# The dense rhythm of the channel-mixing units starts at step 84 instead of step 88

## The chip, the cores and the metric

The kernel runs on one core of a Trainium2 chip. A core has a matrix engine (TensorE, PE in the profile, with its weight loads as PEld), a vector engine (VectorE, DVE), a scalar engine (ScalarE, ACT), a general engine (GpSimd, POOL) and an engine that issues transfers (SyncE, SP). They run side by side and wait for each other through semaphores. Sixteen DMA engines move the data. The metric is the device time of one execution in microseconds.

## What is computed

Three blocks follow each other, for a batch of B = 4 sequences of S = 448 tokens:

```python
attn = softmax(mask(q @ k.T / sqrt(64))) @ v          # 12 heads of 64 columns -> x of 768 columns
h  = relu(x.T @ w_tok1) @ w_tok2                      # token mixing, 448 -> 256 -> 448
u  = x + h.T
x2 = u + relu(u @ w_ch1) @ w_ch2                      # channel mixing, 768 -> 1536 -> 768
theta = x2 @ w_theta                                  # third block
y  = w_tok_r @ (x2 * cos(theta)) + w_tok_i @ (x2 * sin(theta))
out = (x2 + y) + relu((x2 + y) @ w_ch)
```

The inputs are 64-bit floats. Large products are made as three products of a high and a low part (`mm3`, lines 170 to 172), so that little precision is lost.

## The kernel before

**Attention is a loop of 168 steps.** The 12 heads of a batch make 6 pairs, the 4 batches 24 pairs, and a pair has 7 tiles of scores. Step `n` is tile `n % 7` of pair `n // 7`. A step issues `scores` (PE products at L274 and L276, the masked minimum on DVE at L281, the exponential on ACT at L283) and then `late_step(n - 4)`, the product with v of the tile of four steps before.

**The probabilities are transposed in one of two ways.** For pairs 0 to 11 (`NATPV`, steps 0 to 83) PE transposes them through the identity (L290), ACT copies them out of PSUM (L292), and PE multiplies in 32 bits (L318). For pairs 12 to 23 (steps 84 to 167) ACT and DVE split them into two 16-bit parts (tile `ph`, 3 buffers, L111 and L303), SP issues a DMA transpose into tile `pt` (L306), and PE multiplies in 16 bits (L329). PE has less to do in such a step.

**Token mixing.** When two pairs are done, `finish` scales their output and splits it (`xg`, L111 on ACT and L118 on DVE), and one step later `tokmix` runs (L354 to L356, L363, L365, and `mm3` on `wt`). It belongs to the attention's own chain. The last one of a batch makes the columns `acc`, which are split into `ut` for channel mixing.

**Channel mixing is cut into 96 units**, 24 for each batch: 6 units `ch1_unit` and 6 units `ch2_unit` for each half of the 1536 columns. A unit is 18 products of 128x128 by 448 columns (L170 to L172, with `ws` as the weights; `ut` or `h` as the other operand), and its result leaves PSUM through ACT and DVE (L387, L388) or DVE (L396). Units are the filler between the steps of attention: the list `UNIT_STEPS` says behind which step each unit is issued. From unit 0 at step 46 there is one unit each 3 steps (14 in 42), and from step 88 on 29 units in 42 steps. Units that the loop has not issued follow after it: one, then the last token mixing, then all but the last 16, and those between the loading of the third block's weights.

**The weights of a unit** fill a tile `ws` of 768 KB (4 buffers). For units 0 to 23 they must be converted from 64-bit floats first, a *rounding*: SP fetches `raw` (768 KB, 2 buffers, L124), ACT takes the absolute value (L127), DVE assembles the 32-bit value (L134, L135, L137, L138), ACT and DVE split it into `ws` (L111, L118), and SP stores it (`w_c<-ws`, L448). `ROUNDINGS` says at which step: by hand for the even units from 14 on and a few others (`AHEAD_STEPS`, long before their unit), and otherwise at `UNIT_STEPS[n] - 5`, so that the tile goes straight into its unit. A rounding's first part is issued behind the scores of its step, and the rest, the store and the fetch for the next rounding but one, behind those of the step after. All other weights, those of units 24 to 95 among them, are streamed back from memory (`ws<-w_c`, L165) by `load_unit`, called for the next two units after each unit.

```python
        for j, (at_step, _) in enumerate(ROUNDINGS):
            if at_step == n - 1:
                with tc.issue_after(pairs[b, pr].first.ins):
                    round_rest(j)
...
        if n >= LAG:
            with tc.high_priority(AHEAD):
                late_step(n - LAG)
...
        run_units(sum(at_step == n for at_step in UNIT_STEPS))
    for n in range(len(steps) - LAG, len(steps)):
        late_step(n)
    run_units(1)
```

Scores and `late_step` are issued at a high priority. A planner orders the instructions of each engine from the program's order, the priorities and its own costs; on the chip each engine then works in that order.

Of the kernel before, what the change touches and what calls it, by code (L numbers as in the profile page):

```python
# [31 lines left out]
AHEAD, LAG, LOOK = 500, 4, 2  # L32
KEEP, UBACK = 6, 16
LATE_CONVERT = 16
FIRST_UNIT, PHASE, RATES = 46, 42, (14, 29)
UNIT_STEPS = [FIRST_UNIT + -(-n * PHASE // RATES[0]) if n < RATES[0] else
              FIRST_UNIT + PHASE + -(-(n - RATES[0]) * PHASE // RATES[1]) for n in range(72)]
AHEAD_STEPS = {0: 18, 1: 22, 2: 26, 3: 30, 4: 34, 5: 38, 14: 43, 16: 47, 18: 51, 20: 55, 22: 70}
ROUNDINGS = sorted([(at_step, n - 4) for n, at_step in enumerate((3, 4, 8, 9))] +
                   [(AHEAD_STEPS.get(n, UNIT_STEPS[n] - 5), n) for n in range(24)])  # L40
ENGINES = {
# [12 lines left out]
def fused(ctx, tc, q, k, v, w_tok1, w_tok2, w_ch1, w_ch2, w_theta, w_tok, w_ch, out):  # L54
# [353 lines left out]
    def load_unit(n):  # L408
        if n < len(units) and n not in loaded and (n >= 24 or n in stored):
            b, fh, c, t = units[n]  # L410
            loaded[n] = stream_tile(wd[f"c{c}", fh, t])
# [50 lines left out]
    def run_units(n):  # L462
        for _ in range(n):
            u = at[0]
            load_unit(u)
            b, fh, c, t = units[u]
            if c == 1:
                ch1_unit(b, uTs[b], fh, t, loaded[u])
            else:
                ch2_unit(b, uTs[b], accs[b], fh, t, loaded[u])  # L470
            loaded[u] = None
            at[0] += 1
            for ahead in range(LOOK + (u >= 24)):
                load_unit(at[0] + ahead)
            split_ready()
# [31 lines left out]
    for n, (b, pr, t) in enumerate(steps):  # L507
# [27 lines left out]
        if n == FIRST_UNIT - 4:  # L535
            load_unit(0)
            load_unit(1)
        run_units(sum(at_step == n for at_step in UNIT_STEPS))
    for n in range(len(steps) - LAG, len(steps)):
# [247 lines left out]
```

## Time and profile before

| | |
|---|---|
| device time, median of 3 runs | 929.29 us (927.43 to 929.35) |
| profiled execution, span from the first to the last instruction | 924.1 us |
| profiled execution, its own device time | not recorded beside the span; the median lies 5.2 us above the span |
| PE busy | 900.6 us (97%) |
| DVE busy | 633.5 us (69%) |
| ACT busy | 388.2 us (42%) |
| 16 DMA engines, queue of SP | 67.9% |
| mean granted clock of PE | 0.996 of full |

Busy shares are means over the whole span. PE's matmuls are pipelined, so that the duration of one (0.37 us) is longer than its distance to the next (0.20 us). A wait is shown with what released it.

### The profile page before, as it was taken

Reading aid. Unit: us, or ns where it says so; the run is one execution under the profiler, and the core shown is the slowest. Engines: PE = TensorE matmul, PEld = TensorE weight load, DVE = VectorE, ACT = ScalarE, POOL = GpSimd, SP = SyncE. Lnnn points to the kernel's source line nnn. Section 1 sums busy time; section 2 is a strip of 40 time slices with the busy share of each in tenths; the row PEclk is TensorE's granted clock in tenths of the full one; section 3 lists DMA queues with packets and bytes.
Section 4 is the critical chain, followed back from the end, with each engine's and each line's share of the span. In section 5 each row is a group of like instructions: output and inputs, shape, how many; then the busy total and the mean of one; then the engine's idle time right before and its main releaser. Section 6 shows DMA issues by size and latency. Waiting matters only on the chain.

```text
span 924.1 us, 15928 instructions
## 1 busy us (share of the span) xinstructions
PE 900.6 (97%) x5820; PEld 825.6 (89%) x5820; DVE 633.5 (69%) x1468; ACT 388.2 (42%) x914; POOL 109.9 (12%) x177
## 2 busy tenths in 40 slices
PE   7999999997999999999999999999999999999998
PEld 5988999896898898989899999999999999999997
DVE  6799797998987777467774288845864566575341
ACT  6788677675655555344532144321211212202100
POOL 2110000000000000000000000021631233242120
PEclk9999999998999999999999999999999999999999
DMA  6677994789999979699797899864505225054033
GB/s 184 190 254 254 360 335 172 251 300 272 260 316 317 285 207 263 223 275 290 199 322 244 280 326 369 281 195 132 184 1 162 78 86 179 19 162 128 6 133 129
DMA packets 104687, 199.17 MB, mean 216 GB/s; under 512 B 60896, under 2 KB 72992, under 8 KB 104608
## 3 DMA queue, kind: packets, MB, share of 16 engines
q1 hardware_dynamic: 103296, 196.35, 67.9%
q0 software_dynamic: 1152, 1.57, 0.9%
q8 instruction: 46, 0.75, 0.3%
q14 instruction: 33, 0.27, 0.1%
q10 hardware_dynamic: 160, 0.23, 0.1%
HBM read 149.36 MB, written 34.60 MB: 199 GB/s over the span
## 4 chain that ended last, share of the span: by engine, by line
PE 81%; DMA 10%; DVE 6%; issue 1%; ACT 1%; SPq 1%; ACTq 0%; DVEq 0%
PE ps_mm L170 18%; PE ps_mm L172 18%; PE ps_mm L171 18%; DMA pt<-ph 6%; PE ps_sc L274 3%; PE ps_sc L172 3%; PE ps_sc L170 3%; PE ps_sc L171 3%; PE ps_pv L318 3%; PE ps_pv L329 3%; DMA raw<-in_w_ch_dram 2%; PE ps_mm L290 2%; PE ps_sc L276 1%; PE ps_mm L355 1%; PE ps_mm L356 1%
## 5 line engine op out<-in xcount | busy, mean ns | idle before, releaser
L170 PE MATMUL ps_mm<-h,ws 128*128 128x448 f32 x432 | 159.4, 370 | 2.1 <-DMA ws<-w_c 1.3
L171 PE MATMUL ps_mm<-h,ws 128*128 128x448 f32 x432 | 159.2, 369 | 0.0
L172 PE MATMUL ps_mm<-h,ws 128*128 128x448 f32 x432 | 158.6, 368 | 0.0
L172 PE MATMUL ps_mm<-ut,ws 128*128 128x448 f32 x288 | 106.4, 369 | 0.0
L170 PE MATMUL ps_mm<-ut,ws 128*128 128x448 f32 x288 | 106.3, 369 | 0.0
L171 PE MATMUL ps_mm<-ut,ws 128*128 128x448 f32 x288 | 105.9, 368 | 0.0
L283 ACT ACTIVATE sb<-sb,mx 128x192 f32<-128x192 f32 (+3 forms) x168 | 89.3, 532 | 32.4 <-DVE mx L281 31.4
L170 PEld LDWEIGHTS ps_mm<-h,ws 128*128 128x128 f32 x432 | 81.2, 188 | 9.7 <-DMA ws<-w_c 1.6
L172 PEld LDWEIGHTS ps_mm<-h,ws 128*128 128x128 f32 x432 | 81.2, 188 | 7.0
L171 PEld LDWEIGHTS ps_mm<-h,ws 128*128 128x128 f32 x432 | 81.2, 188 | 6.8
L281 DVE CUSTOM_DVE_ANT_0 sb<-ps_sc,mask 128x192 f32<-128x192 f32 (+3 forms) x168 | 74.2, 455 | 10.2 <-PE ps_mm L290 5.8
L114 POOL TENSOR_SCALAR ut<-acc 128x448 fp32r<-128x448 f32 x24 | 17.4, 731 | 474.9 <-PE ps_mm L171 454.3
L591 ACT ACTIVATE tmp<-ps_sc 128x384 f32<-128x384 f32 x28 | 13.5, 482 | 132.3 <-PE ps_sc L172 132.1
L303 DVE SCALAR_TENSOR_TENSOR ph<-sb,ph 128x64 f16<-128x64 f32 (+3 forms) x156 | 42.8, 318 | 33.2 <-ACT ph L111 32.4
L318 PE MATMUL ps_pv<-v_raw,ptf 128*128 128x128 f32 (+1 forms) x456 | 63.6, 275 | 1.4 <-issue 0.9
L318 PEld LDWEIGHTS ps_pv<-v_raw,ptf 128*128 128x128 f32 x456 | 59.6, 192 | 5.7 <-issue 2.3
L111 ACT ACTIVATE ph<-sb 128x192 f16<-128x192 f32 (+3 forms) x84 | 36.5, 443 | 66.9 <-DMA pt<-ph 66.5
L172 PEld LDWEIGHTS ps_mm<-ut,ws 128*128 128x128 f32 x288 | 54.2, 188 | 4.5 <-issue 0.2
L170 PEld LDWEIGHTS ps_mm<-ut,ws 128*128 128x128 f32 x288 | 54.2, 188 | 4.5 <-issue 0.2
L171 PEld LDWEIGHTS ps_mm<-ut,ws 128*128 128x128 f32 x288 | 54.2, 188 | 4.2
L388 DVE SCALAR_TENSOR_TENSOR h<-ps_mm,h 128x448 fp32r<-128x448 f32 x48 | 29.7, 619 | 31.3 <-ACT h L387 31.2
L598 ACT ACTIVATE tmp<-tmp 128x384 f32<-128x384 f32 x28 | 14.7, 526 | 86.0 <-DVE tmp L596 86.0
(152 smaller groups left out, 2113.7 us busy)
## 6 DMA issues: line engine op xcount, KB each, us to landing
ws<-w_c SPq DMA_DIRECT2D x107, 768.0 KB, 5.5
raw<-in_w_ch_dram SPq DMA_DIRECT2D x30, 768.0 KB, 6.3
w_c<-ws SPq DMA_DIRECT2D x30, 768.0 KB, 6.6
q_raw<-in_q_dram SPq DMA_DIRECT2D x16, 448.0 KB, 5.3
k_raw<-in_k_dram SPq DMA_DIRECT2D x16, 448.0 KB, 6.3
v_raw<-in_v_dram SPq DMA_DIRECT2D x24, 288.0 KB, 4.9
x2d<-acc SPq DMA_DIRECT2D x24, 224.0 KB, 4.8
acc<-x2d SPq DMA_DIRECT2D x24, 224.0 KB, 3.6
```

What stands on the lines that cost most here:

```text
L111: nc.scalar.activation(dst, src, AF.Copy, scale=scale)
L170: nc.tensor.matmul(ps, lhsT=ka(a[:, 0]), rhs=kb(b[:, 0]), start=first, stop=False)
L171: nc.tensor.matmul(ps, lhsT=ka(a[:, 0]), rhs=kb(b[:, 1]), start=False, stop=False)
L172: return nc.tensor.matmul(ps, lhsT=ka(a[:, 1]), rhs=kb(b[:, 0]), start=False, stop=last)
L274: nc.tensor.matmul(ps[:, 0:n], lhsT=lhs, rhs=cut(pp.kh), start=True, stop=pp.kl is None)
L281: pp.first = nc.vector.tensor_tensor_reduce(out=dst, in0=src, in1=msk, op0=ALU.add, op1=ALU.min, scale=-0.125, scalar=3.0e38, accum_out=pp ...
L283: pp.last = nc.scalar.activation(sb[:, 0:kk], sb[:, 0:kk], AF.Exp, bias=pp.mx[:, j:j + 1], scale=-1.0, accum_out=pp.sm[:, j:j + 1])
L290: nc.tensor.transpose(pst[:, u * P:(u + 1) * P], full[:, c0 + u * P:c0 + (u + 1) * P], ident)
L303: nc.vector.scalar_tensor_tensor(out=dst, in0=sb[:, c0:c1], scalar=PSC, in1=hi[:, c0:c1], op0=ALU.mult, op1=ALU.subtract)
L318: pp.pv = nc.tensor.matmul(pp.ps[:, reg:reg + n], lhsT=pt[:, u], rhs=pp.v[0][:, vt * D:vt * D + n], start=(u == 0), stop=(u == len(blks) - 1))
L329: pp.pv = nc.tensor.matmul(pp.ps[:, reg:reg + D], lhsT=pt[:, blk], rhs=pp.v[c][:, vt * D:(vt + 1) * D], start=(n == 0), stop=(n == len(job ...
L388: gates[0] = nc.vector.scalar_tensor_tensor(out=t[:, 1], in0=ps[:, 0:S], scalar=0.0, in1=f32v(t[:, 0]), op0=ALU.max, op1=ALU.subtract)
```

## The change

The list of steps is made in another way. The sparse part stays one unit each 3 steps from step 46, now for 13 units; the dense part begins at step 84, the first step of pair 12, and spreads units 13 to 69 evenly over steps 84 to 167.

```diff
-FIRST_UNIT, PHASE, RATES = 46, 42, (14, 29)
-UNIT_STEPS = [FIRST_UNIT + -(-n * PHASE // RATES[0]) if n < RATES[0] else
-              FIRST_UNIT + PHASE + -(-(n - RATES[0]) * PHASE // RATES[1]) for n in range(72)]
+FIRST_UNIT, SPLIT_FROM, STEPS, EVERY = 46, 84, 168, 3
+EARLY = -(-(SPLIT_FROM - FIRST_UNIT) // EVERY)
+UNIT_STEPS = [FIRST_UNIT + n * EVERY if n < EARLY else
+              SPLIT_FROM + (n - EARLY) * (STEPS - SPLIT_FROM) // (70 - EARLY) for n in range(72)]
```

Worked out, the two lists are:

| unit | 0 to 12 | 13 | 14 | 15 | 16 | 17 | 18 | 24 | 48 | 68 | 69 |
|---|---|---|---|---|---|---|---|---|---|---|---|
| step before | 46, 49, ... 82 | 85 | 88 | 90 | 91 | 93 | 94 | 103 | 138 | 167 | after the loop |
| step after | the same | 84 | 85 | 86 | 88 | 89 | 91 | 100 | 135 | 165 | 166 |

| rounding for unit | 13 | 15 | 17 | 19 | 21 | 23 |
|---|---|---|---|---|---|---|
| step before | 80 | 85 | 88 | 91 | 94 | 97 |
| step after | 79 | 81 | 84 | 87 | 90 | 93 |

All other roundings keep their step. The loop issues 70 units instead of 69.

## Rows read from the trace of the kernel before

**Rows 1.** Page, its head.

```profile
span 924.1 us, 15928 instructions
```

**Rows 2.** Waits of PE: waiter, releaser, us in total, times, longest.

```profile
PE ps_pv L329 <- DMA pt<-ph: 6.2, 5, 3.0
...
PE ps_mm L354 <- ACT xg L111: 2.6, 1, 2.6
```

**Rows 3.** Windows: start:end, length, busy time by engine, clock, DMA share, GB/s.

```profile
190.00:200.00 10.00, 10.00 (x71) 9.52 (x70) 9.86 (x21) 8.25 (x19) 0.00 (x0) 1.00 0.73 240
200.00:205.00 5.00, 5.00 (x33) 4.78 (x32) 5.00 (x19) 3.95 (x12) 0.00 (x0) 1.00 0.97 324
205.00:210.00 5.00, 5.00 (x30) 4.71 (x30) 4.66 (x11) 2.14 (x6) 0.00 (x0) 1.00 1.55 266
210.00:215.00 5.00, 2.05 (x27) 1.38 (x26) 2.87 (x7) 3.54 (x6) 0.00 (x0) 1.00 0.71 208
215.00:220.00 5.00, 1.71 (x15) 1.35 (x16) 4.94 (x11) 3.09 (x9) 0.00 (x0) 0.68 1.06 308
220.00:225.00 5.00, 5.00 (x41) 4.90 (x39) 3.55 (x13) 3.66 (x10) 0.00 (x0) 0.64 1.09 344
```

**Rows 4.** Timeline of PE: start, length, instruction, idle time before it.

```profile
211.42 0.20 PE L329 MATMUL ps_pv<-v_raw,pt 128*128 128x64 bf16 x1 [0.62 <-DMA pt<-ph]
...
215.27 0.50 PE L354 MATMUL ps_mm<-xg,wt 128*128 128x256 f32 x2 [2.60 <-ACT xg L111]
...
219.72 0.23 PE L329 MATMUL ps_pv<-v_raw,pt 128*128 128x64 bf16 x1 [3.02 <-DMA pt<-ph]
```

**Rows 5.** Timeline of PE: first product of unit 14, and what follows its eighteenth.

```profile
230.81 0.37 PE L170 MATMUL ps_mm<-ut,ws 128*128 128x448 f32 x1
...
234.45 0.28 PE L274 MATMUL ps_sc<-kh,qs 128*128 128x256 f32 x1
```

**Rows 6.** Timeline of ACT in the same stretch.

```profile
211.46 0.47 ACT L111 ACTIVATE ph<-sb 128x320 f16<-128x320 f32 x1 [4.32 <-DMA pt<-ph]
...
214.61 0.61 ACT L111 ACTIVATE xg<-x 128x512 fp32r<-128x512 f32 x1
```

**Rows 7.** Timeline of SP: issues ahead of the first DMA transposes, and these.

```profile
199.04 0.33 SPq L124 DMA_DIRECT2D raw<-in_w_ch_dram  x1
199.42 0.42 SPq L165 DMA_DIRECT2D ws<-w_c  x1
202.40 0.33 SPq L448 DMA_DIRECT2D w_c<-ws  x1
203.45 7.09 SPq L306 DMA_TRANSPOSE pt<-ph  x3
```

**Rows 8.** Timeline of DVE: the five instructions of one rounding, that of unit 15.

```profile
202.63 0.56 DVE L134 TENSOR_SCALAR wf<-wf 128x768 f32<-128x768 f32 x1
...
203.64 0.56 DVE L135 TENSOR_SCALAR wf<-wf 128x768 uint32<-128x768 uint32 x1
...
205.26 0.96 DVE L137 SCALAR_TENSOR_TENSOR wf<-raw,wf 128x768 uint32<-128x768 uint32 x1
...
206.67 0.95 DVE L138 SCALAR_TENSOR_TENSOR wf<-raw,wf 128x768 uint32<-128x768 uint32 x1
...
212.69 0.96 DVE L118 TENSOR_TENSOR ws<-wf,ws 128x768 fp32r<-128x768 f32 x1 [0.17 <-ACT ws L111]
```

**Rows 9.** DMA issues: count, KB each, median us from issue to landing.

```profile
ws<-w_c SPq DMA_DIRECT2D x107, 768.0 KB, 5.5
...
pt<-ph SPq DMA_TRANSPOSE x84, 5.0
```

**Rows 10.** Timeline after the last token mixing, of DVE and of PE.

```profile
533.38 1.16 DVE L118 TENSOR_TENSOR ut<-acc,ut 128x448 fp32r<-128x448 f32 x2
...
539.55 0.37 PE L170 MATMUL ps_mm<-ut,ws 128*128 128x448 f32 x1
```

**Rows 11.** Window behind the hole, columns as in rows 3.

```profile
225.00:323.00 98.00, 95.84 (x817) 86.17 (x815) 80.90 (x215) 56.32 (x138) 0.00 (x0) 1.00 1.04 295
```

## The prediction

> **What bounds the kernel now.** I read the page first: the span is 924.1 us [rows 1] and PE works 900.6 us of it (table above), so no edit that leaves PE's work alone can win more than the 23.5 us in which PE stands still, plus what a lowered clock costs. This one leaves the work alone; it only moves units 13 to 69 to earlier steps. So the question is where PE stands still, and whether moved units fall there. The waits of PE come next [rows 2]: the longest releaser is the DMA transpose, 6.2 us in 5 waits, and there is one of 2.6 us on the split `xg` that token mixing reads. The windows then show where: from 190 to 210 PE is never idle, from 210 to 220 it works 2.05 + 1.71 = 3.76 of 10 us, and from 220 on it is full again [rows 3]. This is the one hole of size in the whole middle of the kernel. The timeline of PE gives its edges [rows 4]: idle 0.62 us until the first transposed tile (211.42), 2.60 us until `xg` (215.27), 3.02 us until the second transposed tile (219.72), 6.24 us together. They are the first steps of pair 12, the first pair with DMA transposes.
>
> The clock adds to it. It is granted at 0.68 in 215 to 220 and at 0.64 in 220 to 225 [rows 3]. With the two levels 1 and 0.5, that is (0.32 + 0.36) x 2 x 5 = 6.8 us at 1.2 GHz, after the longest idle time began. 3.6 us of them lie behind 220, so the clock is back at about 223.6; PE, idle until 219.72, worked 3.9 us at the low clock, which would have taken half. The low clock costs about 1.9 us. The whole hole is worth 6.2 + 1.9 = 8.1 us. The Trainium skill (TensorE: Matmul & The Clock Gate, Terms) prices throttled time at that time x (1 - 1/2), here 3.4 us, and by it the hole would be worth 9.6; the rows differ, since an engine that waits loses nothing to its clock.
>
> **What the change does there.** In the old list unit 13 comes behind step 85 and unit 14 behind step 88, and step 88 also issues the last token mixing of batch 1. That mixing is the work that waits for `xg`, so in the hole PE has no unit left that stands ahead of it. In the new list units 14 and 15 come behind steps 85 and 86, ahead of that mixing. A unit takes 234.45 - 230.81 = 3.64 us of PE [rows 5], two take 7.3 us: enough for 6.2 us of idle time and 1.1 us more. After that the pace is as before (57 units in 84 steps, 0.68 a step, for 0.69), two or three units ahead all the way. No PE instruction is added or removed.
>
> Unit 14's weights are no obstacle: they are streamed at 199.42 [rows 7], 12 us before the hole. Those of unit 15 must be rounded at steps 81 and 82 instead of 85 and 86, and here is the price.
>
> **The moved rounding on DVE.** One rounding is 0.56 + 0.56 + 0.96 + 0.95 + 0.96 = 4.0 us of DVE [rows 8]. From step 82 on, DVE is one rounding further than before at the same step. DVE is busy 9.86 of 10, 5.00 of 5 and 4.66 of 5 us in 190 to 210 [rows 3], so nothing hides the 4.0 us there: the scores of steps 83 to 88, which ACT, the transposes and `xg` follow, come later by up to 4.0 us. In 210 to 225 DVE has 2.1 + 0.1 + 1.5 = 3.7 us to spare, so most of it is made up by the end of the hole. Bounds: 0.3 us (4.0 less all that spare time) and 4.0 us.
>
> **The moved transfers on SP's queue.** With each rounding go its store and the fetch of a later one, 768 KB each. In the old order the first transposes (issued from 203.45) stand behind the fetch, the stream and the store of 199.04 to 202.40 [rows 7]; ACT gets its `ph` buffer back only at 211.46, after 4.32 us of waiting, and `xg` is queued behind that on ACT until 214.61 [rows 6]. In the new order the store for unit 15 and one more fetch, 1.57 MB, are also issued before step 84. At the 266 GB/s of 205 to 210 [rows 3] they take 5.9 us. Nothing of it is felt if they fit into the idle DMA time of 190 to 200 (share 0.73, 2.7 us to spare), and all of it if they are issued just ahead of the transposes, whose median landing is 5.0 us [rows 9]. Bounds: 0 and 5.9 us. By step 88 a third transfer, the stream of unit 16, is earlier too, another 3.0 us at that rate.
>
> The Trainium skill (DMA: Bandwidth & Descriptors, Queues, rings and completion order) says that SP owns one ring on each of the 16 DMA engines and that descriptors are consumed in ring order, which speaks against this change: a transpose issued after a store begins after it. By that rule alone the attention chain would be late by the full 5.9 us; the 4.32 us wait of ACT behind three such transfers agrees with it.
>
> **The sum.** Let d be the delay of the attention chain (transposes, `xg`, token mixing) at the end of the hole. PE is then 7.3 us of units ahead and d late, and the 1.9 us of the clock are won if the idle time left is short: gain = 7.3 + 1.9 - d, at most 8.1. DVE and DMA are late side by side, not one after the other, so d lies between 0.3 and 5.9; I take 4.0, the whole rounding on DVE, nearer to the full DMA price than to nothing, since both resources are full in 200 to 210. Gain = 9.2 - 4.0 = 5.2 us; with d = 0.3 it is 8.1, with d = 5.9 it is 3.3. From the span of 924.1 this gives 918.9. The median of the runs lies 5.2 us above that span, and I carry this over: 924.1 us, with 921.2 and 926.0 as its own range.
>
> **What costs nothing, and its cover.** Behind the loop one unit less is left to fill. The last token mixing's `ut` split ends at 533.38 + 1.16 = 534.54, and the first unit that needs it starts at 539.55 [rows 10]: 5.0 us of cover, of which the missing unit takes 3.64. The loading of the third block's weights loses the same 3.64 us of cover, but PE has 18 units more there. Where that cover were gone, each would cost what is over, 1 to 3 us. PSUM banks: units 14 and 15 leave through ACT, which waits 4.32 us for a `ph` buffer just there; four banks hold four results, and the cost beyond that would be a new wait of that size.
>
> **The rivals.**
> - *The hole is filled wholly, and the other waits on transposes too.* The waits on transposes sum to 6.2 us [rows 2], 0.62 + 3.02 of them in the hole. With two units in hand PE could cover the other 2.6 us as well: 8.1 + 2.6 = 10.7 us, 918.6. For it: the extra units are always ready work. Against: PE takes its queue in order, and a unit behind a waiting product fills nothing.
> - *Given back.* From 225 to 323 us the DMA engines' mean busy share is 1.04 at 295 GB/s [rows 11], and each unit there needs a tile of 768 KB. Two units ahead means 1.57 MB more by any given time, 5.9 us at 266 GB/s, and if transfers set the pace there, PE waits for them later: gain 8.1 - 5.9 = 2.2 us, less a further dip of the clock of 1.9, about 929. Against: PE works 95.84 of these 98 us, so that DMA, full as it is, mostly keeps up.
> - *Slower: the transposes queue behind the moved transfers.* If a transpose waits for whatever SP issued ahead of it, as ACT's 4.32 us behind three transfers suggest [rows 6, 7], the three that are moved ahead of step 88 are 5.9 + 3.0 = 8.9 us, and if DVE's 4.0 us come before and not beside them, d = 12.9. It decides from d = 9.2 on; at 12.9 the time is 929.3 + 3.7 = 933. For it: share 1.55 in 205 to 210 [rows 3], the highest shown. Against: the store and the fetch are issued around 200, when the queue still has room.
> - *Nothing happens.* The planner could place unit 14 where it stood. The new list puts it three steps ahead of the token mixing in the program, so this is unlikely; 929.3.
>
> **Chances.** My forecast (d from 0.3 to 5.9) 0.54; wholly filled with the other waits too 0.12; given back 0.15; slower by the queue 0.16; nothing 0.03. A change of under 0.2%, 1.9 us, is about what a measurement of this kernel can't tell from none. The first two cases are faster by more than that. Given back splits over faster (0.02), same (0.11) and slower (0.02); nothing is same. Sum: faster 0.68, same 0.14, slower 0.18. The range, 918.5 to 931, leaves out the far end of the queue case; it is wide because cases of both signs hold part of the chance, and 921.2 to 926.0 stands beside it for the likeliest.
>
> **What the profile after would show.** Right: two more units of `ut,ws` products ahead of the last token mixing of batch 1, no idle time of PE over 2 us there, and a granted clock of 1.00 from 205 to 230. The first transposes would be issued 1 to 4 us later than 203.45 against the scores of the step before, with the fifth instruction of unit 15's rounding ahead of them on DVE. Wrong, if the wait of L329 on `pt<-ph` or of L354 on `xg` stays at some 3 us although the two units stand before it (d over 7), if new waits of L170 on `ws<-w_c` appear between 230 and 320 us (given back), or if PE pauses for `ut` behind the last token mixing.

## The result: slower, though the hole is half filled

The changed kernel takes 935.21 us (median of 6 runs, 931.90 to 939.06), the kernel before beside it 928.48 us (922.42 to 931.57). The ratio is 1.0088, with a 95% interval of 1.0069 to 1.0107: slower by 6.7 us in the medians and by some 8 us in the ratio, where 5.2 us of gain were forecast, and outside the range of 918.5 to 931. One point on the metric first: the profiled execution after has a span of 932.2 us and a time of its own of 934.03, so only 1.8 us lie around a span. The 5.2 us that the prediction carried over were mostly something else: at 924.1 + 1.8 = 925.9, the profiled execution of before took 3.4 us less than its median. A second profile of it spans 926.0 us, at a time of 927.74.

The new list takes one line more, so that line numbers are one higher after: L171 is L170 of before. The page after begins with span and busy time by engine:

```profile
span 932.2 us, 15919 instructions
...
PE 903.3 (97%) x5820; PEld 827.2 (89%) x5820; DVE 633.7 (68%) x1468; ACT 388.4 (42%) x914; POOL 109.2 (12%) x177
```

The same 5820 PE instructions, so PE stands still for 932.2 - 903.3 = 28.9 us where it was 23.5. The windows of the hole after, columns as in [rows 3]:

```profile
210.00:215.00 5.00, 3.06 (x27) 2.60 (x25) 4.81 (x13) 2.91 (x6) 0.00 (x0) 1.00 0.97 316
215.00:220.00 5.00, 3.71 (x18) 3.46 (x19) 4.94 (x10) 3.34 (x8) 0.00 (x0) 1.00 1.10 269
220.00:225.00 5.00, 5.00 (x44) 4.53 (x43) 5.00 (x16) 2.90 (x7) 0.00 (x0) 1.00 1.06 396
...
265.00:270.00 5.00, 5.00 (x19) 4.54 (x18) 2.77 (x8) 0.76 (x2) 0.00 (x0) 0.66 0.94 371
...
425.00:430.00 5.00, 4.21 (x45) 3.99 (x46) 3.15 (x11) 3.11 (x9) 0.00 (x0) 0.66 0.97 266
```

From 210 to 220 PE works 3.06 + 3.71 = 6.77 us instead of the 3.76 of [rows 3], and in this execution the clock stays at 1.00. What is lost lies elsewhere, and longer windows show where. Before, four stretches (first column behind the length: PE's busy time):

```profile
205.00:260.00 55.00, 46.66 (x378) 41.85 (x378) 48.93 (x120) 35.40 (x82) 0.00 (x0) 0.94 1.01 272
260.00:345.00 85.00, 84.93 (x738) 77.09 (x737) 64.29 (x180) 44.28 (x109) 0.00 (x0) 1.00 1.01 281
345.00:440.00 95.00, 94.18 (x712) 85.94 (x711) 60.43 (x168) 43.47 (x109) 0.00 (x0) 1.00 0.93 264
440.00:510.00 70.00, 68.67 (x514) 62.88 (x513) 44.18 (x106) 28.71 (x66) 0.00 (x0) 1.00 0.87 259
```

After, the same stretches:

```profile
205.00:260.00 55.00, 51.77 (x418) 46.89 (x417) 52.41 (x132) 35.66 (x83) 0.00 (x0) 1.00 1.01 303
260.00:345.00 85.00, 80.65 (x631) 71.99 (x630) 57.74 (x164) 41.13 (x104) 0.00 (x0) 0.98 0.98 273
345.00:440.00 95.00, 91.05 (x744) 82.76 (x743) 59.70 (x171) 45.15 (x108) 0.00 (x0) 0.98 0.89 234
440.00:510.00 70.00, 67.01 (x508) 61.12 (x507) 47.06 (x111) 30.04 (x71) 0.00 (x0) 1.00 0.89 261
```

In 205 to 260 PE works 51.77 - 46.66 = 5.1 us more, and the 1.9 us of low clock are gone as well. The two profiles can also be set side by side by the work that PE has done, each product counted at its median distance to the next in the kernel before. By that measure the changed kernel is 3.8 us ahead at 225 us and 5.9 ahead at 258. It is level at about 325, 6.1 us behind at 430, 8.6 behind at 500 and 8.1 behind at the end. These are single executions; a second one of each kernel gives the same course, 5.1 us ahead at 258 and 8.3 behind at the end. In 260 to 510 PE stands still for 250 - 80.65 - 91.05 - 67.01 = 11.3 us, where before it was 250 - 84.93 - 94.18 - 68.67 = 2.2. Two stretches of low clock come on top, 0.34 x 2 x 5 = 3.4 us each in the windows above, which cost up to half of that, 1.7 us each. 9.1 + 3.4 = 12.5 of the 14.5 us that are lost between 258 and 500.

The timeline of PE after (start, length, instruction, idle time before it) names the waits:

```profile
213.08 0.19 PE L330 MATMUL ps_pv<-v_raw,pt 128*128 128x64 bf16 x1 [0.61 <-PE ps_sc L277]
...
216.29 0.47 PE L171 MATMUL ps_mm<-ut,ws 128*128 128x448 f32 x1 [2.62 <-DMA ws<-w_c]
...
264.60 0.47 PE L171 MATMUL ps_mm<-h,ws 128*128 128x448 f32 x1 [2.04 <-DMA ws<-w_c]
...
266.02 0.58 PE L171 MATMUL ps_mm<-h,ws 128*128 128x448 f32 x1
266.39 0.58 PE L172 MATMUL ps_mm<-h,ws 128*128 128x448 f32 x1
...
313.80 0.39 PE L275 MATMUL ps_sc<-kh,qs 128*128 128x256 f32 x1 [1.66 <-DVE mx L282]
...
362.77 0.41 PE L275 MATMUL ps_sc<-kh,qs 128*128 128x320 f32 x1 [1.00 <-DVE mx L282]
...
425.79 0.20 PE L330 MATMUL ps_pv<-v_raw,pt 128*128 128x64 bf16 x1 [2.66 <-DMA pt<-ph]
...
499.68 0.44 PE L171 MATMUL ps_mm<-ut,ws 128*128 128x448 f32 x1 [1.27 <-DVE h L389]
```

There is no second hole, and no single resource: a handful of waits of 1 to 3 us, on streamed weights, on the masked minimum of the scores, on a transpose, on a split. The wait at 216.29 is in the hole: unit 14 waits for its weights, against the prediction. In the kernel before, PE's timeline has one more wait on a transpose behind the hole, which the changed kernel doesn't have; its 2.10 us are the step from 3.8 to 5.9:

```profile
245.74 0.20 PE L329 MATMUL ps_pv<-v_raw,pt 128*128 128x64 bf16 x1 [2.10 <-DMA pt<-ph]
```

SP's timeline after shows why unit 14 waits:

```profile
205.31 0.33 SPq L449 DMA_DIRECT2D w_c<-ws  x1
206.35 1.29 SPq L307 DMA_TRANSPOSE pt<-ph  x1
207.75 0.52 SPq L125 DMA_DIRECT2D raw<-in_w_ch_dram  x1
208.44 2.13 SPq L307 DMA_TRANSPOSE pt<-ph  x1
210.62 0.58 SPq L166 DMA_DIRECT2D ws<-w_c  x1
...
211.77 0.38 SPq L449 DMA_DIRECT2D w_c<-ws  x1
```

DVE's timeline after, the split into `ph` for the first transpose and the last instruction of unit 15's rounding:

```profile
205.99 0.30 DVE L304 SCALAR_TENSOR_TENSOR ph<-sb,ph 128x128 f16<-128x128 f32 x1
...
209.56 0.97 DVE L119 TENSOR_TENSOR ws<-wf,ws 128x768 fp32r<-128x768 f32 x1
```

DVE's timeline before, the same split:

```profile
203.10 0.62 DVE L303 SCALAR_TENSOR_TENSOR ph<-sb,ph 128x128 f16<-128x128 f32 x3
```

And ACT's timeline after shows the chain at `xg`:

```profile
216.38 0.65 ACT L112 ACTIVATE xg<-x 128x512 fp32r<-128x512 f32 x1
```

The first transpose is issued at 206.35 instead of 203.45 [rows 7], 2.9 us late, and `xg` starts at 216.38 instead of 214.61 [rows 6], 1.8 us late. The 2.9 us are there already on DVE, where the split ahead of the first transpose starts at 205.99 instead of 203.10. They don't come from the moved transfers on SP's queue: the fetch at 207.75 and unit 15's store at 211.77 are issued behind the first transpose, not ahead of it. And the stream for unit 14, issued at 199.42 before, comes at 210.62. In the new list the rounding for unit 15 begins at step 81. Its second part, which asks for a `ws` buffer, stands in step 82 ahead of the call that loads unit 14 (behind unit 12, in the same step). The kernel asks for its four `ws` buffers in turn, so unit 15 now takes the earlier buffer and unit 14 the next to come free; the experiment below that asks for unit 14's buffer first agrees with it.

### The profile page after: what moved, and what is told of

It reads as the page before. It is cut to its first block, busy times and chain, and to the rows that moved or that the text cites. A ratio compares the mean times of both kernels' runs of the same rounds, so it can differ in the third digit from the quotient of the medians.

```text
span 932.2 us, 15919 instructions
## 1 busy us (share of the span) xinstructions
PE 903.3 (97%) x5820; PEld 827.2 (89%) x5820; DVE 633.7 (68%) x1468; ACT 388.4 (42%) x914; POOL 109.2 (12%) x177
## 4 chain that ended last, share of the span: by engine, by line
PE 74%; DMA 12%; DVE 9%; issue 3%; ACT 2%; SPq 0%; POOL 0%; ACTq 0%; DVEq 0%; POOLq 0%
PE ps_mm L171 17%; PE ps_mm L173 16%; PE ps_mm L172 16%; DMA pt<-ph 7%; PE ps_sc L275 4%; PE ps_sc L173 3%; PE ps_sc L171 3%; PE ps_sc L172 3%; PE ps_pv L319 3%; DMA raw<-in_w_ch_dram 3%; PE ps_pv L330 2%; PE ps_mm L291 2%; DMA ws<-w_c 1%; DVE wf L138 1%; DVE ph L304 1%
## 5 line engine op out<-in xcount | busy, mean ns | idle before, releaser
L171 PE MATMUL ps_mm<-h,ws 128*128 128x448 f32 x432 | 160.1, 371 | 2.9 <-DMA ws<-w_c 2.0
L171 PE MATMUL ps_mm<-ut,ws 128*128 128x448 f32 x288 | 106.3, 369 | 3.9 <-DMA ws<-w_c 2.6
L171 PEld LDWEIGHTS ps_mm<-h,ws 128*128 128x128 f32 x432 | 81.6, 189 | 10.4 <-DMA ws<-w_c 2.2
L171 PEld LDWEIGHTS ps_mm<-ut,ws 128*128 128x128 f32 x288 | 54.3, 188 | 8.6 <-DMA ws<-w_c 2.7
L397 DVE TENSOR_TENSOR acc<-ps_mm,acc 128x448 f32<-128x448 f32 x48 | 29.8, 622 | 37.3 <-PE ps_mm L173 37.1
```

Of the source, the lines that this page charges most:

```text
L171: nc.tensor.matmul(ps, lhsT=ka(a[:, 0]), rhs=kb(b[:, 0]), start=first, stop=False)
L397: nc.vector.tensor_tensor(out=acc[d], in0=ps[:, 0:S], in1=acc[d], op=ALU.add)
```

## The experiments

All are edits of the kernel before, beside the list of units, unless the changed kernel is named. Ratios are to the kernel before on the same chip, with 95% intervals.

**Only the hole.** Units 13 to 15 as in the new list, all others where they stood. `hole_again` is the same kernel once more, and `hole16` moves one unit more, 16 to step 88.

```diff
+UNIT_STEPS[13:16] = [84, 85, 86]        # hole_only, hole_again
+UNIT_STEPS[13:17] = [84, 85, 86, 88]    # hole16
```

> Only units 13, 14 and 15 move (steps 84, 85, 86); unit 16 and all later ones, and their roundings, keep the steps of the kernel before, so the lead of two units is spent by step 91. If the late loss comes from holding the lead (A), the hole shrinks by 5 to 6 us and nothing is lost later: 923 to 926 against 928.5 of before. If the hole only moves to steps 87 to 91 (R), idle time of 3 us or more shows up at 225 to 240 us and the time is that of before within 2 us. If any move of units re-deals the later waits (C), it scatters, 925 to 937, with waits at other places than in the changed kernel.

> Units 13, 14, 15 at steps 84, 85, 86 once more, unaltered. If the gain belongs to the order and not to the chip or the hour, the ratio to before comes again at 0.992 to 0.996 and the hole is closed.

> Units 13 to 16 at steps 84, 85, 86 and 88, all others as before. If the moved steps alone decide, 0 to 2 us better than with three units, 919 to 921. If the dealt order decides (C), anything from 920 to 932, with a closed hole all the same.

`hole_only` took 920.81 us, 0.9936 (0.9912 to 0.9960), and again 924.12 us, 0.9968 (0.9946 to 0.9991): faster than the kernel before, by 3 to 7 us. `hole16` took 931.79 us, 1.0052 (1.0031 to 1.0074). One unit, moved by three steps, costs 7.7 us against `hole_again` beside it, with no rounding moved. Theory A, that the lead itself must be paid for, has `hole_only` right in its direction; `late_only` below goes against it. The windows of `hole_again`:

```profile
210.00:215.00 5.00, 4.48 (x36) 3.78 (x34) 4.13 (x14) 2.93 (x7) 0.00 (x0) 1.00 0.87 295
215.00:220.00 5.00, 4.25 (x21) 3.79 (x21) 4.94 (x11) 4.65 (x11) 0.00 (x0) 1.00 1.15 292
...
260.00:345.00 85.00, 85.00 (x700) 76.98 (x699) 61.95 (x171) 46.51 (x113) 0.00 (x0) 1.00 1.04 293
345.00:440.00 95.00, 93.56 (x780) 85.47 (x779) 66.53 (x183) 49.04 (x121) 0.00 (x0) 1.00 0.87 255
440.00:510.00 70.00, 69.79 (x486) 63.80 (x485) 41.84 (x100) 25.53 (x56) 0.00 (x0) 1.00 0.91 276
```

The windows of `hole16`:

```profile
260.00:345.00 85.00, 77.65 (x666) 69.17 (x665) 61.18 (x171) 43.67 (x109) 0.00 (x0) 0.98 0.97 275
```

Two units in the hole leave PE idle 10 - 4.48 - 4.25 = 1.3 us of 6.2, and 1.7 us in 260 to 510: the gain of the forecast is there when little is lost later. In the profile of `hole_only`, the same kernel, it is 0.9 us in the hole and 4.6 us in 260 to 510, so that some 3 us behind the hole differ between two executions of one order. `hole16` loses 7.35 us in 260 to 345 alone. Its hole isn't closed as expected either: PE works 2.99 and 3.71 us in the two windows, at a clock of 0.73 in the second. The timeline of SP in `hole_again`:

```profile
211.33 1.07 SPq L165 DMA_DIRECT2D ws<-w_c  x2
```

The timeline of PE there:

```profile
215.35 0.39 PE L274 MATMUL ps_sc<-kh,qs 128*128 128x256 f32 x1 [0.51 <-DVE mx L281]
216.25 0.47 PE L170 MATMUL ps_mm<-ut,ws 128*128 128x448 f32 x1 [0.40 <-DMA ws<-w_c]
```

The stream of unit 14 is as late here as in the changed kernel, and unit 14 begins at the same time, 216.25. But scores stand ahead of it in PE's order, so that it waits 0.40 us and not 2.62. The late stream becomes a wait only with the order around it.

**The other parts of the list.** `lead_back`: units 13 to 23 as in the new list, the rest as before. `late_only`: units 13 to 23 as before, the new list from 29 on, and a bridge between them. `late_plus1`: before, with every unit from 24 on a step later.

```diff
+UNIT_STEPS[13:24] = [84 + (n - 13) * 84 // 57 for n in range(13, 24)]    # lead_back
+UNIT_STEPS[24:29] = [103, 103, 104, 104, 106]                            # late_only
+UNIT_STEPS[29:] = [84 + (n - 13) * 84 // 57 for n in range(29, 72)]
+UNIT_STEPS[24:] = [x + 1 for x in UNIT_STEPS[24:]]                       # late_plus1
```

> Units 13 to 23 and their roundings as in the changed kernel, units 24 to 71 as in the kernel before: the lead is held through the roundings and given up at steps 98 to 103. A: the gain of 5 to 6 us at 258 us stays, less the wait for a streamed weight tile near 262 us (2.0 us and 1.7 us of clock) if the dense roundings cause it (B): 923 to 927. C: anything between 925 and 937.

> Units 0 to 23 as before; two units are moved ahead at steps 103 to 106 and units 29 to 71 stand where the changed kernel has them. There is no gain in the hole, only the lead after it. A: it loses what the changed kernel loses from 280 us on, 6 to 10 us: 935 to 939. C: scatter, 926 to 937. If the loss is due to the dense roundings alone (B), it stays at 928.5 within 2 us.

> Units 0 to 23 as before, units 24 to 71 one step later: a move of the same kind the other way, with one unit more behind the loop. A: no loss, 927 to 930, or a small gain as the filler stands later. C: scatter like that of the changed kernel, 926 to 937, with new waits of 1 to 3 us at places of their own.

929.36 us, 1.0029 (1.0013 to 1.0046); 929.04 us, 1.0020 (1.0003 to 1.0036); 933.30 us, 1.0054 (1.0033 to 1.0075). All three lose, and the two parts of the new list lose less than the whole of it (1.0088). `late_plus1` does the reverse of the change from unit 24 on, later instead of earlier, and loses 5 us as well. So a lead of units that must be paid back later doesn't explain the loss by itself: with the lead alone `late_only` was to take 935 to 939 us by theory A. `lead_back`, which has the dense roundings, lies above the 923 to 927 of A and B, inside the wide band of C. `late_only` fits B and C alike.

**A fourth `ph` buffer**, in the kernel before and in the changed one, since ACT waits 4.32 us for one in the hole [rows 6].

```diff
-BUFS = dict(ut=9, h2=6, acc=12, ws=4, wf=2, raw=2, sb=3, ph=3, pt=5)
+BUFS = dict(ut=9, h2=6, acc=12, ws=4, wf=2, raw=2, sb=3, ph=4, pt=5)
```

> The kernel before with a fourth ph buffer: what the buffer is worth there. P: the hole at 211 to 220 us shrinks, since ACT's 4.3 us wait ahead of xg goes, and the time falls by 2 to 5 us, to 923 to 926. Q or C: within 2 us of 928, with waits at other places.

> The changed kernel with a fourth ph buffer, so that ACT may run one tile further ahead of the DMA transposes. If the later waits come from ACT and DVE standing behind a transpose that still holds its ph buffer (P), the waits on pt<-ph and on the scores' minimum between 255 and 500 us go down and the time falls to 924 to 930. If they come from the order of the transfers on SP's queue (Q), or from the re-dealt order alone (C), it stays at 932 to 938.

930.61 us, 1.0045 (1.0026 to 1.0064), and 926.36 us, 0.9996 (0.9978 to 1.0014). The same buffer costs the one kernel 4 us and gives the other some 9 us. For the changed kernel this is the time that P gave, and PE's waits on the scores' minimum fall from 3.9 to 2.2 us; but those on `pt<-ph`, which P had fall too, stay at 4.2 us for 4.1. For the kernel before P gave 923 to 926, and it got slower. The edit deals out the order anew as well, so what the buffer itself is worth stays open.

**Streams on a queue of their own.** During attention the weights `ws<-w_c` are issued by POOL instead of SP, so that no transpose stands behind one of them in SP's queue. It tests one part of the rival by which transposes queue behind moved transfers: the streams leave SP's queue, while the stores and fetches of the roundings stay in it.

```diff
-        nc.sync.dma_start(out=f32v(w), in_=kept)
+        (nc.gpsimd if att_on[0] else nc.sync).dma_start(out=f32v(w), in_=kept)
```

> The kernel before with the streamed tiles issued from POOL: what the queue is worth without the lead. Q: a gain of 0 to 4 us, less than in the changed kernel, 924 to 928. C: scatter within 925 to 934.

> The changed kernel with the streamed weight tiles (ws from w_c, 1 to 48 of them during attention) issued from POOL, which is idle there, so that they stand neither ahead of nor behind the DMA transposes on SP. Q: the waits on ws at 213 and 262 us go, those on pt shrink, and the time falls to 922 to 928. P or C: 931 to 938.

952.02 to 965.12 us, 1.0355 (1.0295 to 1.0416), and 948.80 to 965.98 us, 1.0311 (1.0218 to 1.0404), four runs each: both lose some 3%, and no theory had that. The waits of PE in the changed kernel with this edit (releaser: us in total, times, longest):

```profile
PE ps_pv L330 <- DMA pt<-ph: 22.9, 9, 9.2
```

With all transfers in SP's queue these waits are 4.1 us in the changed kernel, and 6.2 [rows 2] against 15.1 in the kernel before. The median landing of a transpose goes from 4.9 to 5.5 us, and from 5.0 to 5.7. The Trainium skill (DMA: Bandwidth & Descriptors, Issuing engines are not separate DMA queues) says that transfers of all issuing engines run on the same 16 engines and interleave, so that another queue saves only the time of issuing. That the transposes don't gain agrees with it; a loss of 3%, with one transpose waited for by 9.2 us, is more than it says. So taking the streams out of SP's queue is no cure. The order of instructions changes with this edit too, and the page of the profile counts POOL's streams as another kind of queue (software_dynamic), so the 3% can't be put to the place in a queue alone.

**The weights of unit 14 earlier.** The changed kernel and `hole_only`, with `load_unit(14)` called at step 79, ahead of the rounding for unit 15.

```diff
-        if n == FIRST_UNIT - 4:
-            load_unit(0)
-            load_unit(1)
+        for u in {79: (14,), FIRST_UNIT - 4: (0, 1)}.get(n, ()):
+            load_unit(u)
```

> The changed kernel with the stream of unit 14's weights issued at step 79 instead of behind unit 12 at step 82, so that it takes its buffer ahead of the roundings of units 13 and 15. If unit 14's late weights hold the rest of the hole (W), the 2.6 us wait on ws at 216 us goes, and the lead at 258 us grows from 6 to 8 us; the end gains 2 to 4 us, 930 to 934, since the later waits stay. If the order that the planner deals sets the later waits (C), the end may move by 5 us or more either way whatever the hole does.

> Units 13, 14, 15 at steps 84, 85, 86, all others as before, and unit 14's stream issued at step 79. W: the hole is filled with nothing left, 0 to 2 us better than without the early stream, 918 to 921. C: the time moves by some us either way, 918 to 927.

The changed kernel with it: 924.11 us, 0.9966 (0.9948 to 0.9985), 11 us quicker than without. `hole_only` with it: 928.86 us, 1.0013 (0.9996 to 1.0031), 4 to 7 us slower than without by the ratios, where both theories had it at 927 or less. The changed kernel with the early load, its timeline of SP:

```profile
190.50 0.38 SPq L166 DMA_DIRECT2D ws<-w_c  x1
```

Its windows:

```profile
210.00:215.00 5.00, 5.00 (x28) 4.60 (x27) 4.57 (x14) 2.49 (x6) 0.00 (x0) 1.00 0.84 317
215.00:220.00 5.00, 5.00 (x56) 4.56 (x55) 4.94 (x10) 5.00 (x12) 0.00 (x0) 1.00 0.70 157
...
260.00:345.00 85.00, 83.96 (x699) 75.89 (x698) 61.26 (x173) 44.14 (x112) 0.00 (x0) 1.00 1.09 290
345.00:440.00 95.00, 91.50 (x719) 82.47 (x718) 61.27 (x171) 43.79 (x106) 0.00 (x0) 1.00 0.89 244
440.00:510.00 70.00, 68.22 (x517) 62.11 (x516) 45.91 (x109) 30.64 (x71) 0.00 (x0) 1.00 0.90 253
```

In 210 to 220 PE now never stands still, and the wait for unit 14's weights is gone. At 225 us this kernel is 7.1 us ahead of the one before, where the changed one is 3.8 ahead. But it waits at 227.54 and 231.04 for 0.74 and 1.72 us, the second time for a transpose, and at 258 us it is 5.9 us ahead, exactly as the changed one is. The difference of 932.2 - 923.8 = 8.4 us between the two spans lies behind it, in 260 to 510: 250 - 83.96 - 91.50 - 68.22 = 6.3 us idle against 11.3, and no low clock against 3.4 us of cost. Same list of units, same lead at 258, another outcome. Even so this kernel's profile is back level with the one before at 500 us: it gives back its 5.9 us, where the changed one loses 14.5.

**One step, one unit.** The kernel before with unit 17 a step earlier, and its rounding with it (`nudge17`), or with unit 18 a step later, whose rounding is set by hand and stays (`nudge18`).

```diff
+UNIT_STEPS[17] = 92    # nudge17, was 93
+UNIT_STEPS[18] = 95    # nudge18, was 94
```

> The kernel before with one unit, 17, one step earlier (92 for 93), its rounding with it: no lead, no density to speak of. If the lead or the density costs the time (A or B), it stays within 1 us of before. If any re-dealing of the order costs, as the kernel before stands in an order that fits (C), it moves by 2 to 6 us, mostly up, with new waits on transposes at 300 to 480 us.

> As the last, with unit 18 one step later (95 for 94), and no rounding moved. A or B: within 1 us of before. C: 2 to 6 us either way, mostly up, and not the same as for unit 17.

931.81 us, 1.0053 (1.0037 to 1.0069), and 927.82 us, 0.9999 (0.9982 to 1.0017). A single unit, one step, no lead to speak of: 5 us as C had it in the one case, and nothing, as A and B had it, in the other. Two gaps of PE in `nudge17`, of the same kinds as in the changed kernel:

```profile
286.59 0.39 PE L274 MATMUL ps_sc<-kh,qs 128*128 128x256 f32 x1 [1.38 <-DVE mx L281]
...
317.48 0.22 PE L329 MATMUL ps_pv<-v_raw,pt 128*128 128x64 bf16 x1 [3.10 <-DMA pt<-ph]
```

In the records of PE, compared one by one, `nudge17` and the kernel before have a different PE instruction (by line and tiles) at 735 of 5820 places, all between 216 and 336 us: one step of one unit makes the planner deal out the order anew for 120 us. In this stretch the loss lies: from 225 to 336 PE is idle for 5.5 us, for 2.2 in the kernel before, and from 336 to 510, where the order is the old one, for 1.6 and 2.2. `hole16` has the old order again from 374 us on; it is idle for 7.4 us against 2.4 from 225 to 375, and for 1.4 against 1.9 from there to 510. `nudge18` differs at 601 places, between 259 and 374, and loses nothing. So a new order needn't cost; some do.

**Is it the order or the execution?** Both kernels once more, for a second profile.

> The kernel before once more: the hole at 211 to 220 us comes again with its 6.2 us, and behind 258 us there is again little idle time, 4 us or less.

> The changed kernel once more, unaltered, for a second profile. If the late waits belong to its order (C), the waits on ws at 216 and 264 us, on the scores' minimum at 314, on pt at 425 and on the units at 480 to 500 come again within 1 us of their place and half of their size. If they belong to the execution, they are at other places and the sum differs by 5 us or more.

927.74 us and 936.08 us. The kernel before has its hole again (10 - 2.73 - 1.90 = 5.4 us idle in 210 to 220, a clock of 0.68 and 0.64 in 215 to 225) and 1.3 us of idle time in 260 to 510. The timeline of the changed kernel's second execution:

```profile
217.62 0.74 PE L171 MATMUL ps_mm<-ut,ws 128*128 128x448 f32 x1 [3.06 <-DMA ws<-w_c]
...
268.60 0.47 PE L171 MATMUL ps_mm<-h,ws 128*128 128x448 f32 x1 [2.39 <-DMA ws<-w_c]
...
316.03 0.39 PE L275 MATMUL ps_sc<-kh,qs 128*128 128x256 f32 x1 [1.49 <-DVE mx L282]
...
365.26 0.42 PE L275 MATMUL ps_sc<-kh,qs 128*128 128x320 f32 x1 [1.02 <-DVE mx L282]
...
428.75 0.24 PE L330 MATMUL ps_pv<-v_raw,pt 128*128 128x64 bf16 x1 [1.56 <-DMA pt<-ph]
```

The same waits come 1 to 4 us later, which is more than the expected 1 us, and mostly of like size. The one at 499.68 comes at 501.27 with 0.83 us and another releaser, and one of 1.13 us at 335.14 is new. PE is idle for 10.4 us in 260 to 510, where the first execution had 11.3, and its 5820 instructions stand in the same order in both. So most of these waits belong to the order of instructions, not to the accident of one execution. The low clock isn't as steady: in 260 to 345 it shows in the first execution and not in the second, and in the hole it is the other way round:

```profile
215.00:220.00 5.00, 2.38 (x6) 2.15 (x7) 4.97 (x10) 4.00 (x9) 0.00 (x0) 0.60 1.14 317
```

**The planner without its simulated times.** Both kernels ordered by program and priorities alone.

```diff
-    with tile.TileContext(nc, schedule_with_timeline_sim=True) as tc:
+    with tile.TileContext(nc, schedule_with_timeline_sim=False) as tc:
```

> The kernel before with its instructions left in the order of program and priorities, without the planner's simulated times. Some slower than before, 930 to 960; the hole at pair 12 is there too.

> The changed list in the same way. If the moved steps themselves fill the hole and cost nothing (C: only the dealt order costs), it is 4 to 8 us faster than before_noplan. If the lead or the denser roundings cost by themselves (A or B), it is the same or slower by up to 8 us, as with the planner.

994.76 us, 1.0707 (1.0675 to 1.0739), and 1002.57 us, 1.0803 (1.0769 to 1.0836), both beyond what was expected. The changed list is 1002.57 / 994.76 = 1.0079 times as long here too, a loss of 7.8 us where theory C, the order dealt anew by the planner, had the changed list win. Its strong form falls: a loss of this size also comes without the simulated times. What the pair can't say is whether it is the same loss: by the waits of PE, those on `mx` rise from 9.8 to 16.4 us and those on `ws` from 10.6 to 15.9, while those on `pt` fall from 22.2 to 18.5, all over a kernel that is 7% slower. There too PE's idle time falls in 205 to 260, from 12.1 to 9.3 us, and rises in 260 to 510, from 28.9 to 31.0. The runs of the two, four each, overlap (990.58 to 1001.72 and 998.75 to 1005.11 us).

## Why the prediction was wrong

**The hole: right in the main, and in part by luck.** Its place and the direction of d came out, and units 14 and 15 fill it by half, with PE idle for 3.2 us instead of 6.2. All of unit 14 and 13 products of unit 15 stand ahead of the last token mixing of batch 1, but for the first product of that mixing. d was 1.8 us at `xg` and 2.9 at the first transpose, where 4.0 was taken between 0.3 and 5.9. At the first transpose it came over DVE and not over the queue: the store and the fetch that were to delay it by up to 5.9 us went out behind it. The lead of 5.9 us at 258, beside the 5.2 of the sum, is luck: 3.8 us of it stand at 225, where the sum ends, and 2.1 are the wait at 245.74, which only the rival of the wholly filled hole had counted. Of the signs of being right, three did not hold: PE has an idle time of 2.62 us there, the last instruction of unit 15's rounding comes behind the split for the first transpose, and the clock of 1.00 is that of the first execution alone.

**"Unit 14's weights are no obstacle: they are streamed at 199.42": wrong.** I took the time of a stream from the trace of before without asking which step of the list had put it there. The moved rounding took the buffer that the stream had had, the stream came 11.2 us later, and unit 14 waited 2.62 us (3.06 in the second execution). With the load at step 79 the wait is gone. But `hole_only` and `hole_again` win with a stream as late, and with the early load the lead at 258 us is no greater: the 11 us that this load wins are not those of the wait, and lie behind 258 us.

**"After that the pace is as before": this is the step that failed.** The sum ends at 225 us and takes everything behind it as unchanged, at a cost of nothing. In fact 14.5 us are lost between 258 and 500, in waits of 1 to 3 us for four kinds of releaser, with two stretches of low clock behind such waits. At 264.60 it can be followed in the rows: 2.04 us of waiting, then products 0.37 us apart instead of 0.20 while the clock is at 0.66, 3.4 us at 1.2 GHz with PE busy all the time. The Trainium skill (TensorE: Matmul & The Clock Gate, Terms) would charge half of that, an estimate of 1.7 us; with PE busy throughout, the trace agrees: products 0.37 us apart instead of 0.20 give 3.4 x (1 - 0.20 / 0.37) = 1.6 us.

**The rivals.** "Given back" had the shape, a filled hole and a later loss, and its sign, a new wait on `ws<-w_c` between 230 and 320 us, came at 264.60. But at 5.9 + 1.9 us it was sized at about half, and its mechanism, transfers that set the pace for two units of lead, is not borne out as the whole of it. `after_early14` has the same lead and loses 8.4 us less (6.3 us idle and a steady clock), three of the five late waits shown are on DVE and not on a transfer, and the DMA share behind the hole is no higher after (0.98 and 0.89) than before (1.01 and 0.93). "Slower by the queue" falls with d under 3 us, where it needed 9.2, and with the place of store and fetch behind the first transpose. "Nothing happens" falls with the order: unit 14 did move.

**What the runs support in its place** is that the time behind the hole hangs on the particular order of instructions, which the list of units only sets indirectly. Small edits that should be neutral or mild moved the kernel by up to 11 us, in either direction: one unit by one step 0 or +5 us, one more unit in the hole +8, one more buffer +4 or -9, one earlier load -11 or +5. Most of the waits recur in a second execution of the same kernel, and `nudge17` and `hole16` lose only where their order differs from that of before. The kernel before is among the orders with hardly any late wait: PE is idle in 260 to 510 for 2.2 and 1.3 us in its two executions, for 2.8 in `nudge18`, for 1.7 and 4.6 in the two of `hole_again` and `hole_only`, and for 4.7 (`late_only`) to 11.3 us in every other list, load or `ph` count that was tried. So a re-dealt order has more to lose there than to win. Neither list is bad as such: with one more buffer or one earlier load the new list takes no longer than the old.

**What stays open.** Which decision of order makes each late wait was not isolated. `after_early14` changes both the stream and the order behind it, so how much of its 11 us is either can't be told. And the pair without simulated times, which loses the same 0.8%, may mean that the new list has a cost of its own that the other edits happened to cover; no run rules that out. Three kernels with the whole new list lose behind 258 us, against the one before: the changed one 14.5 us, with the early load 6.0, with a fourth `ph` buffer 4.8. This fits such a cost; but `hole16` and the kernel before with that buffer lose 10.4 and 9.0 without the new list.

## What to carry to other kernels

Fill a hole with the few units that fill it, leave the rest of the list alone, and time the neighbours: three changed entries gave 3 to 7 us, four lost 4, fifty-seven lost 6.7. For any step that is moved, ask in which order the buffers are taken after the move; a time read for a stream in the old trace is a result of the old order. Where a planner deals out the order anew, a forecast from the old trace held here up to the place of the edit and not behind it: add an uncertainty of the size that one-step edits show (here some 0.5%), and try such neighbours before a cause is put to a result of that size.

## What the runs showed of the hardware

With the streams moved to POOL's queue beside DMA transposes on SP's queue both kernels took some 3% longer, and in the changed one a product waited 9.2 us for its transpose; with all in one queue its longest such wait was 2.7 us. The order of instructions differed as well. And waits as short as 2.0 to 2.7 us on PE, at 264.60 and 425.79, each came with about 3.4 us at half clock in one execution of the changed kernel, while the wait of 2.62 us at 216.29 in the same execution did not. In the second execution, with PE's instructions in the same order, it was the other way: the clock fell to 0.60 in 215 to 220 with the wait of 3.06 us at 217.62, and stayed at 1.00 behind that of 2.39 us at 268.60.
